# Attention into an MLP on one core: q and k of two batches turned to token slots before a full-width transpose, and the beacon keys of a batch by one operation

## The chip, the cores and the metric

The kernel runs on 1 core of one Trainium2 chip. The metric is the device time of one launch in microseconds (us); the median of 3 runs before the change is 348.35 us (348.26 to 348.68). The engines of a core are TensorE (PE), VectorE (DVE), ScalarE (ACT), GpSimd (POOL) and SyncE (SP), the last used here to issue DMAs. POOL issues DMAs too, those that convert fp32 to bf16 on the way among them.

## The reference

Attention over 8 batches, 8 heads, 576 tokens of 64 elements, with 16 beacon keys and values ahead of the token keys, which every query may see; the token part is causal. The result, as 4608 tokens of 512, goes through an MLP with a squared ReLU.

```python
k_all = np.concatenate([beacon_k, k], axis=2)          # 16 + 576 keys
v_all = np.concatenate([beacon_v, v], axis=2)
scores = scale * np.matmul(q, k_all.transpose(0, 1, 3, 2))
causal[:, Nb:] = np.triu(np.ones((S, S), dtype=bool), k=1)
scores = np.where(causal, -1000000000.0, scores)
a = softmax(scores)
x = np.matmul(a, v_all)                                # then (B*S, H*D)
h = x @ w_in
r = np.maximum(h, 0.0)
out = (r * r) @ w_out
```

## The kernel before

Every step is a small operation (`Op`) with a name, the engine or engines that may run it, a planned duration, a priority and the operations that it needs. When the kernel is built, a planner (`Order.run`) plays them through: whenever an engine is free it starts the ready operation with the lowest priority number. What comes out is one fixed order per engine. On the chip each engine keeps its order and waits by semaphores. The planner also deals out PSUM's 8 banks in classes with limits (`tp`, the transposes, has 2 banks at most), staging buffers `stg` (8), and buffers `pt` (4) for the exponentials. It adds 0.096 us where PE changes between "full", "rows" and "columns" operations (`mode`).

The work of a batch goes by pairs of heads, `pr` = 0 to 3:

- Keys and queries are needed with the 64 elements of a head on partitions, two heads of a pair on 128: `kT` and `qT`. In batches 0 to 2 (`b < NPE`), `add_strided` makes them on PE. POOL's DMAs (line 463) put k and q as bf16 into `ks` and `qs`, parts of `qk_area`: 96 partitions, and on each partition 6 token slots per head (token = 6 x partition + slot). A `tp` operation then transposes, for k and for q, each slot of each head by itself (line 480): 96x64 in, 64x96 out, the second head to the upper 64 partitions, 24 matmuls a pair, mode "columns". Line 476 adds the pair's beacon keys. `ek` (VectorE) copies keys and beacon keys to `kT`, `eq` (VectorE or ScalarE) copies `qT`, bringing the tokens back in order.
- The beacon keys are loaded for all heads by SP (line 445) and cast by VectorE (line 448), in `add_beacon`.
- From batch 3 on, q and k are loaded by SP to `stg`, cast by POOL and transposed by DMA. Ahead of batches 3 and 4 POOL clears parts of `qk_area` (lines 381 and 382), once the transposes of batches 1 and 2 are read out.
- `qk` (line 584) multiplies keys and queries in two row halves of the array, ScalarE takes the exponential (line 597), VectorE masks by `tri` (lines 607 and 611), `av` (line 627) multiplies by the values `vb`, VectorE normalises to `xn` (lines 642 and 643). Of batch 1, the value loads are issued by POOL, not SP.
- `xT` is the transpose of `xn`, by PE in batches 0 and 1 (line 691), by DMA later.
- The MLP runs in 9 chunks of 512 tokens: line 755 (w_in), relu on ScalarE (772) or VectorE (774), square on VectorE (781), line 792 (w_out), a copy by ScalarE to `osb` (355), and SP's store. MLP matmuls have high priority numbers, so they fill PE when no attention operation is ready. A gate holds a pair's attention back until the MLP is far enough along.

Line 357 is the helper `copy_on`, through which copies and casts of VectorE and POOL go. The weights are loaded by POOL: `w_in` (716) before batch 1's q and k, `w_out` (725) after batch 1's values.

Of the kernel before, what the change touches and what calls it, by code (L numbers as in the profile page):

```python
# [9 lines left out]
FP32 = mybir.dt.float32  # L10
BF16 = mybir.dt.bfloat16
# [77 lines left out]
class Order:  # L89
# [147 lines left out]
def kernel(  # L237
# [11 lines left out]
    nc = tc.nc  # L249
    B, H, S, D = q.shape  # L250
    Nb = beacon_k.shape[2]
    HP = H // 2
# [14 lines left out]
    def sb(name, shape, dt):  # L267
        return pool.tile(shape, dt, name=name)
# [5 lines left out]
    stg = [sb(f"stg{i}", [128, H, D], FP32) for i in range(NSTG)]  # L274
    NP = 96
    NS = S // NP
# [25 lines left out]
    ps = psum.tile([128, 8, 512], FP32, name="ps")  # L302
# [4 lines left out]
    def bank(op, k=0):  # L307
        return ps[:, op.held[k], :]
# [19 lines left out]
    add = order.add  # L328
# [16 lines left out]
    ident_op = add("ident", "POOL", 0.6, lambda e: make_identity(nc, ident), prio=-199.8)  # L345
# [7 lines left out]
    def copy_on(e, dst, src):  # L353
        if e == "ACT":
            nc.scalar.copy(dst, src)  # L355
        else:
            eng[e].tensor_copy(dst, src)  # L357
# [3 lines left out]
    cast = {}  # L361
    trans = {}
    qk_ops = {}
# [77 lines left out]
        deps += [o for p in range(HP * (b - 2), HP * (b - 1)) for o in qk_ops[p]]  # L441
        trans[b, x] = [add(f"tr{b}{x}", "SP", 3.8, emit, prio=prio, deps=deps, dma=3.2)]

    def add_beacon(b, prio):
        ld = add(f"bkl{b}", "SP", 0.65, lambda e: [nc.sync.dma_start(
            out=bkf[b % 2], in_=beacon_k[b].transpose([1, 0, 2]))], prio=prio, dma=0.1,
                 deps=[cast[b - 1, "bk"]] if b else [])
        cast[b, "bk"] = add(f"bkc{b}", "DVE", 0.4, lambda e: nc.vector.tensor_copy(bks[b % 2], bkf[b % 2]), prio=prio,
                               deps=[ld])
        return cast[b, "bk"]  # L450

    def add_strided(b, prio):
        loads = {}
        bk = add_beacon(b, prio)
        after = [w_ops["in", 3]] if b == 1 else [strided[b - 1][HP - 1, "q"]] if b else []
        free = trans[b - 2, "q"] + trans[b - 2, "k"] if b >= 2 else []
# [12 lines left out]
        strided[b] = loads  # L469
        for pr in range(HP):  # L470
            h = slice(2 * pr, 2 * pr + 2)
            box = {}

            def emit_tp(e, pr=pr, h=h, box=box):
                pp = pair(box["t"]).bitcast(BF16)
                nc.tensor.transpose(pp[:, 1, 0:Nb], bks[b % 2][:, h, :], ident[0:Nb, 0:Nb])  # L476
                for half, at, t in ((1, Nb, ks), (0, 0, qs)):
                    for u in range(NS):
                        for hj in range(2):
                            nc.tensor.transpose(pp[64 * hj:64 * hj + 64, half, at + u * NP:at + (u + 1) * NP],  # L480
                                                t[b % 2][:, 2 * pr + hj, u, :], ident[0:NP, 0:NP])
# [21 lines left out]
            trans[b, "q"].append(eq)  # L503


    class Phase:
# [397 lines left out]
```

## Time and profile before

| | |
|---|---|
| median of 3 runs | 348.35 us (348.26 to 348.68) |
| the profiled execution | 349.44 us, span 347.7 us |
| granted TensorE clock | 1.00 |
| line 480, half-width transposes | 288 matmuls |
| line 476, beacon transposes | 12 matmuls |
| DMA | 49.50 MB, HBM 134 GB/s over the span |

The span runs from the first to the last instruction that the profile shows; the time of a run has some 1.7 us more around it. Busy time of PE is a sum of overlapping matmuls taken together; the distance from start to start tells what a matmul takes up on the engine. In a timeline a row merges neighbours of one kind: start, time from the first start to the last end, engine, line, operation, shape and count. A releaser in brackets is what ended the engine's idle time before that row.

### The profile page before, as it was taken

The numbers are of one execution on the slowest core, as the hardware profiler recorded it, in microseconds if no ns is written. First come the engines' busy times: TensorE is split into PE (matmuls) and PEld (weight loads), VectorE is DVE, ScalarE is ACT, GpSimd is POOL, SyncE is SP. The second block draws the span as 40 slices with busy tenths as digits, with TensorE's granted clock in tenths as the row PEclk, the third lists the DMA queues.
The fourth block names the chain that finished last, engine by engine and source line by source line (L and its number), as shares of the span: only waits on it lengthen the run. The fifth ranks groups of instructions, "written<-read, shape, count | busy, mean of one in ns | idle before, by whom it ended". The sixth has DMA issues, their size and how long they took to land.

```text
span 347.7 us, 7270 instructions
## 1 busy us (share of the span) xinstructions
PE 331.8 (95%) x2944; PEld 177.7 (51%) x2980; DVE 150.2 (43%) x306; ACT 202.3 (58%) x311; POOL 84.8 (24%) x132
## 2 busy tenths in 40 slices
PE   3799999999999999999999999999999999999995
PEld 2568765554544444544446874454454444444442
DVE  5466683448722464256523772266323302301300
ACT  2678893497854775577655765677536416614611
POOL 8273740357242046105520452000000000000000
PEclk9999999999999999999999999999999999999999
DMA  7989999899978999899986999750014011011002
GB/s 99 188 126 205 221 206 215 192 248 213 201 150 194 208 207 204 130 237 201 238 173 135 215 242 227 120 139 2 3 60 128 2 60 60 2 60 60 3 15 105
DMA packets 137010, 49.50 MB, mean 142 GB/s; under 512 B 123344, under 2 KB 132048, under 8 KB 136976
## 3 DMA queue, kind: packets, MB, share of 16 engines
q1 hardware_dynamic: 127472, 40.09, 55.7%
q0 software_dynamic: 9504, 8.95, 16.0%
q8 instruction: 23, 0.38, 0.5%
q14 instruction: 11, 0.09, 0.1%
HBM read 37.22 MB, written 9.44 MB: 134 GB/s over the span
## 4 chain that ended last, share of the span: by engine, by line
PE 92%; DMA 3%; issue 2%; ACT 1%; DVE 1%; POOL 0%; SPq 0%; ACTq 0%; POOLq 0%
PE ps L755 36%; PE ps L792 36%; PE ps L627 9%; PE ps L584 8%; DMA stg<-in_v_dram 2%; PE ps L480 1%; DMA qk_area<-in_q_dram 1%; PE ps L691 1%; ACT pt L597 1%; DVE pt L607 1%; PE ps L476 0%; DVE g L774 0%; POOL vb L357 0%; ACT osb L355 0%; POOL qk_area L463 0%
## 5 line engine op out<-in xcount | busy, mean ns | idle before, releaser
L755 PE MATMUL ps<-xT,w_in 128*128 128x512 bf16 (+3 forms) x688 | 132.8, 340 | 1.2 <-issue 0.5
L792 PE MATMUL ps<-w_out,g 128*128 128x512 bf16 x556 | 127.8, 379 | 2.0 <-issue 1.4
L597 ACT ACTIVATE pt<-ps 128x832 bf16<-128x832 f32 (+4 forms) x128 | 103.8, 869 | 43.9 <-PE ps L584 41.9
L755 PEld LDWEIGHTS <-w_in 128*128 128x128 bf16 x704 | 65.1, 98 | 56.1 <-issue 5.3
L772 ACT ACTIVATE g<-ps 128x512 bf16<-128x512 f32 (+2 forms) x128 | 71.7, 560 | 36.0 <-PE ps L755 34.7
L792 PEld LDWEIGHTS <-g 128*128 128x128 bf16 x576 | 53.9, 98 | 66.7 <-issue 4.8
L781 DVE TENSOR_TENSOR g<-g 128x1024 bf16<-128x1024 bf16 (+2 forms) x80 | 51.8, 649 | 71.8 <-ACT g L772 71.0
L355 ACT COPY osb<-ps 128x512 f32<-128x512 f32 x36 | 21.1, 587 | 47.4 <-PE ps L792 41.5
L357 POOL CAST vb<-stg 128x512 bf16<-128x512 f32 (+1 forms) x38 | 26.8, 714 | 78.2 <-DMA stg<-in_v_dram 74.0
L607 DVE TENSOR_TENSOR pt<-pt,tri 128x1024 bf16<-128x1024 bf16 (+1 forms) x36 | 24.8, 693 | 45.4 <-ACT pt L597 44.0
L357 POOL CAST qk_area<-stg 128x512 bf16<-128x512 f32 (+2 forms) x50 | 33.2, 676 | 28.2 <-DMA stg<-in_k_dram 14.8
L627 PEld LDWEIGHTS <-pt 128*128 128x128 bf16 (+1 forms) x960 | 34.9, 100 | 8.6 <-issue 1.6
L627 PE MATMUL ps<-vb,pt 128*128 128x65 bf16 (+1 forms) x960 | 36.8, 197 | 1.0 <-POOL vb L357 0.5
L584 PE MATMUL ps<-qT,kT 64*128 64x80 bf16 (+6 forms) x400 | 36.4, 291 | 1.0 <-ACT pt L597 1.0
L774 DVE TENSOR_SCALAR g<-ps 128x512 bf16<-128x512 f32 (+2 forms) x32 | 19.6, 612 | 19.3 <-PE ps L755 18.9
L643 DVE TENSOR_TENSOR xn<-ps,rcp 128x640 bf16<-128x640 f32 (+2 forms) x36 | 27.0, 751 | 1.3
L584 PEld LDWEIGHTS <-kT 64*128 64x128 bf16 x400 | 13.0, 97 | 21.1 <-issue 17.5
L642 DVE RECIPROCAL rcp<-ps 128x10 f32<-128x10 f32 (+2 forms) x36 | 7.6, 211 | 32.4 <-PE ps L627 32.2
L355 ACT COPY qT<-ps 128x576 bf16<-128x576 bf16 x12 | 7.8, 651 | 11.2 <-PE ps L480 11.2
L480 PE MATMUL ps<-ident,qk_area 96*64 96x96 bf16 x288 | 11.1, 233 | 2.7 <-DMA qk_area<-in_q_dram 1.2
L357 DVE COPY kT<-ps 128x16 bf16<-128x16 bf16 (+1 forms) x24 | 9.9, 453 | 5.2 <-PE ps L480 5.0
L480 PEld LDWEIGHTS <-qk_area 96*64 96x64 bf16 x288 | 8.6, 126 | 4.0 <-DMA qk_area<-in_q_dram 2.1
(31 smaller groups left out, 57.2 us busy)
## 6 DMA issues: line engine op xcount, KB each, us to landing
out_dram<-osb SPq DMA_DIRECT2D x17, 512.0 KB, 3.2
stg<-in_v_dram SPq DMA_DIRECT2D x21, 256.0 KB, 5.7
stg<-in_q_dram SPq DMA_DIRECT2D x20, 256.0 KB, 4.9
stg<-in_k_dram SPq DMA_DIRECT2D x15, 256.0 KB, 5.1
w_in<-in_moe_w_in_dram POOLq DMA_DIRECT2D x4, 512.0 KB, 8.7
w_out<-in_moe_w_out_dram POOLq DMA_DIRECT2D x4, 512.0 KB, 10.9
stg<-in_v_dram SPq DMA_DIRECT2D x7, 224.0 KB, 5.2
qk_area<-in_k_dram POOLq DMA_DIRECT2D x4, 288.0 KB, 12.4
```

What stands on the lines that cost most here:

```text
L355: nc.scalar.copy(dst, src)
L357: eng[e].tensor_copy(dst, src)
L480: nc.tensor.transpose(pp[64 * hj:64 * hj + 64, half, at + u * NP:at + (u + 1) * NP], t[b % 2][:, 2 * pr + hj, u, :], ident[0:NP, 0:NP])
L584: nc.tensor.matmul(st[:, hj, at:at + t1 - t0], kT[b % 2][hp, pr, 128 * c:128 * c + 128], qT[b % 2][hp, pr, t0:t1], start=True, stop=True,)
L597: nc.scalar.activation(pt[take_pt.held[0]][:, :, off:off + width], pair(box["qk"], k)[:, :, 0:width], AF.Exp, bias=0.0, scale=scale)
L607: nc.vector.tensor_tensor(out=d, in0=d, in1=tri[:, m0:m0 + m, :][:, None].to_broadcast([128, 2, m, 128]), op=ALU.min)
L627: nc.tensor.matmul(a[:, hj, (t - tl[0]) * (D + 1):(t - tl[0] + 1) * (D + 1)], P[0:rr, hj, o:o + 128], vb[b % 2][0:rr, c, h, :], start=(c = ...
L643: nc.vector.tensor_tensor(out=xn[b % 2].rearrange("p t (h d) -> p h t d", d=D)[:, 2 * pr:2 * pr + 2, tl[0]:tl[0] + nt], in0=a[:, :, :, 0:D ...
L755: nc.tensor.matmul(h[:, lo - spans[0][0]:hi - spans[0][0]], w_in_sb[:, mc, ft * 128:(ft + 1) * 128], xT[:, mc, lo % RING:lo % RING + hi - lo],
L772: nc.scalar.activation(dst, h, AF.Relu, bias=0.0, scale=1.0)
L781: nc.vector.tensor_tensor(out=d, in0=d, in1=d, op=ALU.mult)
L792: nc.tensor.matmul(o, G[:, fc, ts * 128:(ts + 1) * 128], w_out_sb[:, fc, :], start=(fc == 0), stop=(fc == NFT - 1))
```

## The change

Three things change in `add_beacon` and `add_strided`.

1. In batches 1 and 2, VectorE rearranges k and q of each pair before the transpose (`spin`): from head, slot, element to slot, head, element, so that one slot of both heads lies in 128 neighbouring columns. The target is a spare buffer for pair 0 and, for the others, the place of the pair before, which has been rearranged by then. PE then transposes a slot of both heads at once: 12 matmuls of 96x128 instead of 24 of 96x64, mode "full". Batch 0 keeps the 24.
2. The beacon keys of all four pairs of a batch are turned by one operation `tpb` on PE: four matmuls of the 128-row buffer `bks` (rows beyond 16 are zero, by a memset at the start) against 16 columns of the identity, into one PSUM bank. `ekb` copies all of it to `kT` at once. `ek` has no beacon copy any more.
3. Batch 0's beacon keys are staged in a `stg` buffer, loaded by SP and cast by VectorE as before. Those of batches 1 and 2 are loaded by POOL with the conversion in the DMA, into the one `bks`; the load waits for the batch before to be transposed, and stands between the batch's first k and q loads.

The planned durations of `tp` and `ek` change accordingly.

```diff
-    bkf = [sb("bkf", [Nb, H, D], FP32)] * 2
-    bks = [sb(f"bks{i}", [Nb, H, D], BF16) for i in range(2)]
+    bks = sb("bks", [128, H, D], BF16)
+    spare = {x: sb(f"spare{x}", [NP, NS * 2 * D], BF16) for x in "kq"}
...
+    nc.vector.memset(bks, 0.0)
...
-    def add_beacon(b, prio):
-        ld = add(f"bkl{b}", "SP", 0.65, lambda e: [nc.sync.dma_start(
-            out=bkf[b % 2], in_=beacon_k[b].transpose([1, 0, 2]))], prio=prio, dma=0.1,
-                 deps=[cast[b - 1, "bk"]] if b else [])
-        cast[b, "bk"] = add(f"bkc{b}", "DVE", 0.4, lambda e: nc.vector.tensor_copy(bks[b % 2], bkf[b % 2]), prio=prio,
-                               deps=[ld])
-        return cast[b, "bk"]
+    def add_beacon(b, prio, behind):
+        if b == 0:
+            def emit_load(e):
+                return [nc.sync.dma_start(out=stg[ld.held[0]][0:Nb], in_=beacon_k[b].transpose([1, 0, 2]))]
+
+            ld = add(f"bkl{b}", "SP", 0.65, emit_load, prio=prio, dma=0.1, take=("stg", "stg", [1]))
+            bk = add(f"bkc{b}", "DVE", 0.4, lambda e: nc.vector.tensor_copy(bks[0:Nb], stg[ld.held[0]][0:Nb]),
+                     prio=prio, deps=[ld], give=ld)
+        else:
+            bk = add(f"bkl{b}", "POOL", 0.65, lambda e: [nc.gpsimd.dma_start(
+                out=bks[0:Nb], in_=beacon_k[b].transpose([1, 0, 2]))], prio=prio + 0.05, dma=0.1,
+                behind=behind, deps=[tpb_ops[b - 1]])
+        box = {}
+
+        def emit_tpb(e):
+            for pr in range(HP):
+                nc.tensor.matmul(bank(box["t"])[:, Nb * pr:Nb * pr + Nb], bks[:, 2 * pr:2 * pr + 2, :],
+                                 ident[:, 0:Nb], start=True, stop=True)
+
+        def emit_ekb(e):
+            nc.vector.tensor_copy(kT[b % 2][:, :, 0:Nb],
+                                  bank(box["t"])[:, 0:HP * Nb].rearrange("p (g n) -> p g n", n=Nb))
...
+        tpb = add(f"tpb{b}", "PE", 0.2, emit_tpb, prio=100.0 * HP * b - 195, deps=[bk, ident_op] + busy,
+                  take=("ps", "tp", [1]))
...
+        ekb_ops[b] = add(f"ekb{b}", "DVE", 0.14, emit_ekb, prio=-201.0, deps=[tpb], give=tpb)
...
+                    def emit_spin(e, h=h, x=x, t=t, blocks=blocks):
+                        copy_on(e, blocks[x].rearrange("p s (h d) -> p h s d", h=2), t[b % 2][:, h])
+
+                    spin[x].append(add(f"spin{b}{x}{pr}", "DVE", 0.45, emit_spin, prio=prio + pr,
+                                       deps=[loads[pr, x]] + spin[x][-1:] + ([tps[b - 1, 0]] if pr == 0 and b > 1 else [])))
...
-                nc.tensor.transpose(pp[:, 1, 0:Nb], bks[b % 2][:, h, :], ident[0:Nb, 0:Nb])
...
-                        for hj in range(2):
-                            nc.tensor.transpose(pp[64 * hj:64 * hj + 64, half, at + u * NP:at + (u + 1) * NP],
-                                                t[b % 2][:, 2 * pr + hj, u, :], ident[0:NP, 0:NP])
+                        cols = slice(at + u * NP, at + (u + 1) * NP)
+                        if b:
+                            nc.tensor.transpose(pp[:, half, cols], blocks[x][:, u, :], ident[0:NP, 0:NP])
+                        else:
+                            for hj in range(2):
+                                nc.tensor.transpose(pp[64 * hj:64 * hj + 64, half, cols],
+                                                    t[b % 2][:, 2 * pr + hj, u, :], ident[0:NP, 0:NP])
...
-            tp = add(f"tp{b}.{pr}", "PE", 1.0 if b else 1.3, emit_tp, prio=100.0 * (HP * b + pr) - 190,
-                     deps=[bk, loads[pr, "k"], loads[pr, "q"], ident_op] + busy, take=("ps", "tp", [2]), mode="columns")
+            tp = add(f"tp{b}.{pr}", "PE", 0.55 if b else 1.0, emit_tp, prio=100.0 * (HP * b + pr) - 190,
+                     deps=([spin["k"][pr], spin["q"][pr]] if b else [loads[pr, "k"], loads[pr, "q"]]) + [ident_op] + busy,
+                     take=("ps", "tp", [2]), mode="full" if b else "columns")
...
-                copy_on(e, kT[b % 2][:, pr, 0:Nb], pp[:, 1, 0:Nb])
...
-            ek = add(f"ek{b}.{pr}", "DVE", 0.85, emit_k, prio=-200.0, deps=[tp])
+            ek = add(f"ek{b}.{pr}", "DVE", 0.7, emit_k, prio=-200.0, deps=[tp])
...
-            qk_deps = [trans[b, "k"][pr], trans[b, "q"][pr]]
+            qk_deps = [trans[b, "k"][pr], trans[b, "q"][pr], ekb_ops[b]]
```

More of the change, by code (lines that the diff above doesn't have):

```diff
@@ L442, in add_trans @@
         trans[b, x] = [add(f"tr{b}{x}", "SP", 3.8, emit, prio=prio, deps=deps, dma=3.2)]
-    def add_beacon(b, prio):
-        ld = add(f"bkl{b}", "SP", 0.65, lambda e: [nc.sync.dma_start(
-            out=bkf[b % 2], in_=beacon_k[b].transpose([1, 0, 2]))], prio=prio, dma=0.1,
-                 deps=[cast[b - 1, "bk"]] if b else [])
-        cast[b, "bk"] = add(f"bkc{b}", "DVE", 0.4, lambda e: nc.vector.tensor_copy(bks[b % 2], bkf[b % 2]), prio=prio,
-                               deps=[ld])
-        return cast[b, "bk"]
+    tpb_ops = {}
+    ekb_ops = {}
+    def add_beacon(b, prio, behind):
[17 more added lines that the diff above has]
+                                  bank(box["t"])[:, 0:HP * Nb].rearrange("p (g n) -> p g n", n=Nb))
+        busy = [o for pr in range(HP) for o in qk_ops[HP * (b - 2) + pr]] if b >= 2 else []
+        tpb = add(f"tpb{b}", "PE", 0.2, emit_tpb, prio=100.0 * HP * b - 195, deps=[bk, ident_op] + busy,
+                  take=("ps", "tp", [1]))
+        box["t"] = tpb
+        tpb_ops[b] = tpb
+        ekb_ops[b] = add(f"ekb{b}", "DVE", 0.14, emit_ekb, prio=-201.0, deps=[tpb], give=tpb)
     def add_strided(b, prio):
         loads = {}
-        bk = add_beacon(b, prio)
         after = [w_ops["in", 3]] if b == 1 else [strided[b - 1][HP - 1, "q"]] if b else []
+        add_beacon(b, prio, after)
         free = trans[b - 2, "q"] + trans[b - 2, "k"] if b >= 2 else []
@@ L469, in add_strided @@
         strided[b] = loads
+        spin = {"k": [], "q": []}
         for pr in range(HP):
@@ L472, in add_strided, with block @@
             box = {}
-            def emit_tp(e, pr=pr, h=h, box=box):
+            def block(x):
+                if pr == 0:
+                    return spare[x][:, :].rearrange("p (s w) -> p s w", s=NS)
+                return (ks if x == "k" else qs)[b % 2][:, 2 * pr - 2:2 * pr].rearrange(
+                    "p h s d -> p (h s d)").rearrange("p (s w) -> p s w", s=NS)
+            blocks = {x: block(x) for x in "kq"}
+            if b:
+                for x, t in (("k", ks), ("q", qs)):
+                    def emit_spin(e, h=h, x=x, t=t, blocks=blocks):
+                        copy_on(e, blocks[x].rearrange("p s (h d) -> p h s d", h=2), t[b % 2][:, h])
+                    spin[x].append(add(f"spin{b}{x}{pr}", "DVE", 0.45, emit_spin, prio=prio + pr,
+                                       deps=[loads[pr, x]] + spin[x][-1:] + ([tps[b - 1, 0]] if pr == 0 and b > 1 else [])))
@@ L475, in emit_tp @@
+            def emit_tp(e, pr=pr, h=h, box=box, blocks=blocks):
                 pp = pair(box["t"]).bitcast(BF16)
-                nc.tensor.transpose(pp[:, 1, 0:Nb], bks[b % 2][:, h, :], ident[0:Nb, 0:Nb])
-                for half, at, t in ((1, Nb, ks), (0, 0, qs)):
+                for half, at, x, t in ((1, Nb, "k", ks), (0, 0, "q", qs)):
                     for u in range(NS):
-                        for hj in range(2):
-                            nc.tensor.transpose(pp[64 * hj:64 * hj + 64, half, at + u * NP:at + (u + 1) * NP],
-                                                t[b % 2][:, 2 * pr + hj, u, :], ident[0:NP, 0:NP])
+                        cols = slice(at + u * NP, at + (u + 1) * NP)
+                        if b:
+                            nc.tensor.transpose(pp[:, half, cols], blocks[x][:, u, :], ident[0:NP, 0:NP])
[3 more added lines that the diff above has]
+                                                    t[b % 2][:, 2 * pr + hj, u, :], ident[0:NP, 0:NP])
@@ L486, in add_strided @@
+            tps[b, pr] = tp
             box["t"] = tp
@@ L503, in add_strided @@
             trans[b, "q"].append(eq)
+    tps = {}
     class Phase:
```

## The prediction

> **What bounds the kernel now.** I read the page first, for the share of each engine and the chain that ended last.
>
> ```profile
> span 347.7 us, 7270 instructions
> PE 331.8 (95%) x2944; PEld 177.7 (51%) x2980; DVE 150.2 (43%) x306; ACT 202.3 (58%) x311; POOL 84.8 (24%) x132
> PE   3799999999999999999999999999999999999995
> PE 92%; DMA 3%; issue 2%; ACT 1%; DVE 1%; POOL 0%; SPq 0%; ACTq 0%; POOLq 0%
> ```
>
> TensorE (PE) is busy for 331.8 of 347.7 us, the chain is 92% PE, and only the first two slices and the last show PE idle. From about 20 us on the kernel is a queue of TensorE work. What shortens that queue should arrive at the end; what lengthens another engine costs only where PE has to wait for it.
>
> The change touches three stretches: batch 0 at the start, batch 1's transposes around 37 to 45 us, batch 2's around 63 to 74 us. So I cut the span into windows (columns: PE, weight loads, DVE, ACT, POOL busy us; granted clock; DMA share; GB/s).
>
> ```profile
> 8.70:17.40 8.70, 6.67 (x96) 4.41 (x92) 3.81 (x11) 5.78 (x9) 1.84 (x3) 1.00 1.01 188
> 26.00:35.00 9.00, 8.98 (x122) 7.77 (x122) 5.76 (x18) 7.39 (x17) 3.20 (x4) 1.00 1.27 205
> 35.00:46.00 11.00, 11.00 (x171) 7.79 (x170) 8.14 (x20) 9.63 (x20) 8.20 (x13) 1.00 1.17 219
> 46.00:57.00 11.00, 10.89 (x133) 6.41 (x133) 7.33 (x18) 7.88 (x13) 1.79 (x3) 1.00 1.27 204
> 57.00:68.00 11.00, 10.89 (x154) 6.55 (x154) 4.92 (x10) 4.16 (x7) 3.20 (x5) 1.00 1.04 206
> ```
>
> PE is full in all but the first of these, at full clock. VectorE (DVE), to which the change gives work, has 11.00 - 8.14 = 2.86 us free in 35 to 46 us, its busiest stretch, and about 6 us in 57 to 68.
>
> **What one transpose of a pair costs now.** The timeline of PE around the first two of batch 1 (start, time from first start to last end, engine, line, shape, count):
>
> ```profile
> 35.76 1.21 PE L755 MATMUL ps<-xT,w_in 128*128 128x272 bf16 x9
> 36.89 0.18 PE L476 MATMUL ps<-ident,bks 16*128 16x16 bf16 x1
> 37.00 0.70 PE L480 MATMUL ps<-ident,qk_area 96*64 96x96 bf16 x24
> 37.63 1.56 PE L755 MATMUL ps<-xT,w_in 128*128 128x272 bf16 x12
> ...
> 39.24 0.70 PE L480 MATMUL ps<-ident,qk_area 96*64 96x96 bf16 x24
> 39.87 0.38 PE L584 MATMUL ps<-qT,kT 64*128 64x496 bf16 x2
> ```
>
> Starts, not ends, give the price, since matmuls overlap. The two L755 groups differ by 3 matmuls and 0.35 us, so one follows the other by 0.117 us, and one lasts 1.21 - 8 x 0.117 = 0.27 us. The last of the nine therefore starts at 35.76 + 0.94 = 36.70, and the next full-array matmul could have started at 36.82. The beacon transpose starts at 36.89, 0.07 to 0.09 late. It takes a slot of 0.11 us, until 37.00. From there to the next L755 at 37.63 are 0.63 us. A pair's transpose thus keeps PE for 37.63 - 36.82 = 0.81 us.
>
> Of the 0.63 us, the 24 half-width transposes need this much (min/median/max ns of one; L691 for later):
>
> ```profile
> L627 PE MATMUL ps<-vb,pt x420: 190/194/262, 14.5 to 109.8; 128*128 128x65 bf16 x140
> L480 PE MATMUL ps<-ident,qk_area x288: 206/206/290, 4.5 to 73.7; 96*64 96x96 bf16 x144
> ...
> L691 PE MATMUL ps<-ident,xn x40: 199/218/313, 16.7 to 68.5; 128*128 128x128 bf16 x24, 112*128 112x112 bf16 x8, 80*128 80x80 bf16 x8
> ```
>
> (0.70 - 0.206)/11 = 0.045 us for each of 12 steps, so two heads' halves already go side by side. 12 steps are 0.54 us; the remaining 0.09 us at the way out, like that at the way in, stands where PE goes from full-width to 64-column work and back.
>
> **The same transposes in full width.** No row shows 96x128. Two neighbours do, both full-width, each with its own 128-column weight load: 65 moving columns and 128.
>
> ```profile
> 51.30 1.08 PE L627 MATMUL ps<-vb,pt 128*128 128x65 bf16 x30
> ...
> 31.29 1.39 PE L755 MATMUL ps<-xT,w_in 128*128 128x240 bf16 x12
> 32.52 0.31 PE L691 MATMUL ps<-ident,xn 128*128 128x128 bf16 x3
> 32.74 0.47 PE L755 MATMUL ps<-xT,w_in 128*128 128x240 bf16 x3
> ```
>
> L627: (1.08 - 0.194)/29 = 0.0306 us a step. L691 from its start to the next group's: 0.22/3 = 0.073 at most, and about 0.056 a step if the last lasts its shortest 0.199. So 12 transposes cost between 0.37 us (12 x 0.0306) and 0.88 us (12 x 0.073). I take 96 columns midway between 65 and 128, 0.043 us a step, 0.52 us, close to the 0.045 of L480's pairs. L691's transposes also show no lost time beside L755: the last of the 12 before them starts near 32.42, and they follow after 0.10 us, a normal step.
>
> So the transpose of a pair goes from 0.81 to 0.52 us: 0.29 us less, eight times. Two of the eight have a row-split matmul (L584) as a neighbour, the one at 39.24 above and this one:
>
> ```profile
> 72.70 0.48 PE L584 MATMUL ps<-qT,kT 64*128 64x336 bf16 x8
> 73.11 0.18 PE L476 MATMUL ps<-ident,bks 16*128 16x16 bf16 x1
> ```
>
> There one switch of about 0.09 us stays. Gain: 8 x 0.29 - 2 x 0.09 = 2.14 us. The beacon keys of a batch come back as four full-width matmuls with 16 columns; the nearest row is L627's 0.031 us, so 0.12 us a batch, 0.25 us for two (0 to 0.43 if each costs today's 0.11 less the switch). **PE queue: 1.9 us shorter** (1.0 longer with 0.073 a step, 3.1 shorter with 0.0306).
>
> The Trainium skill (TensorE: Matmul & The Clock Gate, section on LDWEIGHTS) says that a weight load takes the number of its columns over 1.2 GHz, whatever the rows; that is 107 ns for 128 columns, and 12 loads would be 1.28 us, an estimate by that page; its section on Fast Weight Load makes such loads about twice as fast. L627's 30 steps of 0.0306 us, each with 128 columns, speak against it here; what it would do is a rival below.
>
> **VectorE's new work.** 16 copies of 96 x 768 bf16 between SBUF buffers, two per pair, one each for k and q. Nearest rows, by shape (count | busy us, mean ns):
>
> ```profile
> L357 DVE COPY kT<-ps 128x16 bf16<-128x16 bf16 x12 | 1.9, 160 | 5.2 <-PE ps L480 5.0
> L448 DVE CAST bks<-bkf 16x512 bf16<-16x512 f32 x3 | 1.3, 420 | 1.5 <-DMA bkf<-in_beacon_k_dram 1.5
> L357 DVE COPY xT<-ps 128x576 bf16<-128x576 bf16 x3 | 1.4, 454 | 2.1 <-PE ps L691 2.1
> L357 DVE COPY xT<-ps 128x240 bf16<-128x240 bf16 x3 | 0.7, 271 | 0.0
> L357 DVE CAST vb<-stg 128x512 bf16<-128x512 f32 x1 | 0.4, 429 | 1.0 <-DMA stg<-in_v_dram 1.0
> ```
>
> The xT copies give (454 - 271)/336 = 0.54 ns an element over 0.14 us fixed, so 0.56 us for 768; the cast fits that line (0.42). If bf16 inside SBUF goes at twice that pace it is 0.35 us. I take 0.45, with 0.35 and 0.56 as ends: 3.6 us a batch. Taken away: four beacon copies of 0.16 us a batch and a 0.42 us cast; added: one 64-column copy, about 0.18 us. In 35 to 46 us VectorE would then have 8.14 + 3.6 - 0.6 + 0.2 = 11.3 us if every copy fell there. They need not:
>
> ```profile
> 35.92 0.74 POOL L402 DMA_DIRECT2D stg<-in_v_dram  x1 [0.61 <-DMA qk_area<-in_q_dram]
> 7.49 1.39 PE L480 MATMUL ps<-ident,qk_area 96*64 96x96 bf16 x24 [1.19 <-DMA qk_area<-in_k_dram]
> 63.16 0.18 PE L476 MATMUL ps<-ident,bks 16*128 16x16 bf16 x1
> ```
>
> POOL's first row shows batch 1's first q in place before 35.92 us, so its copies can use the 3.24 idle us of 26 to 35 as well as the 3.67 of 46 to 57. The planner that writes the order books the copies and fills PE with L755 and L792 work meanwhile. Behind a copy in VectorE's queue stand relu (L774), square (L781), mask (L607) and the kT copies; PE, ScalarE and PSUM banks wait for those. I charge 0.4 us for places where PE stands (0 to 1.9, all of the gain).
>
> **Batch 0 and the queues.** The beacon cast comes behind a new memset, and the first pair waits until the beacon's bank is read. The second row above covers it: PE stands 1.19 us before the second pair anyway, and a delay of that length costs nothing. Without that cover it would cost its length. The beacon load of batch 1 leaves SP's queue ahead of batch 0's v loads: 32 KB at 188 GB/s, 0.17 us off a DMA-bound start at best; I book 0. Two beacon loads move into POOL's queue, between a k and a q load, each pushing the later q and k loads, then v (batch 1) and w_out, by the same 0.2 us; POOL's issue costs another 0.7 us each, while it waits for landings anyway. Batch 2's beacon load also waits for batch 1's beacon matmuls, which stand ahead of batch 1's transposes (36.89); behind it in POOL's queue are batch 2's q and k loads, first used at 63.16, and then the v casts. I book 0 (-0.2 to +0.5).
>
> **Sum.** -1.9 + 0.4 = -1.5 us. The profiled execution took 349.44 us with its span of 347.7, so 1.7 lie around the span; it becomes 347.9. The median of the runs is 348.35, 1.1 lower; the same cut gives 346.8.
>
> **Rivals.** *Given back at PE.* The order is fixed; PE cannot pass a transpose whose copy is late. 1.9/8 = 0.24 us of waiting at each pair eats the gain: 348.3. For it: VectorE's 8.14 of 11, and two copies in a row per pair. Against: the planner books them, and PE was idle for only 0.11 us in each window of 46 to 68.
>
> *Slower: VectorE and GpSimd block each other.* Rows of both engines:
>
> ```profile
> 39.11 2.23 POOL L725 DMA_DIRECT2D w_out<-in_moe_w_out_dram  x3 [1.24 <-DMA qk_area<-in_q_dram]
> 41.32 1.95 POOL L357 CAST vb<-stg 128x512 bf16<-128x512 f32 x3
> 41.45 0.79 DVE L781 TENSOR_TENSOR g<-g 128x480 bf16<-128x480 bf16 x1
> 46.87 0.39 DVE L781 TENSOR_TENSOR g<-g 128x480 bf16<-128x480 bf16 x1
> ...
> 74.79 0.69 DVE L607 TENSOR_TENSOR pt<-pt,tri 128x1024 bf16<-128x1024 bf16 x1 [0.23 <-ACT pt L597]
> 75.59 6.12 POOL L357 CAST qk_area<-stg 128x512 bf16<-128x512 f32 x10
> 80.18 2.08 DVE L607 TENSOR_TENSOR pt<-pt,tri 128x1024 bf16<-128x1024 bf16 x1
> ```
>
> Under POOL's casts a square takes 0.79 instead of 0.39 us and a mask 2.08 instead of 0.69. If each copy is stretched by the same 0.4 us to 0.85, batch 1's eight are 6.8 us: 8.14 + 6.8 - 0.4 = 14.5 in 11, 3.5 over; what 26 to 35 doesn't take stalls relu and squares, and PE. With 3 us lost and 1.9 gained it is 349.5. It decides from (2.86 + 0.4)/8 = 0.41 us a copy if all fall into that window, from about 0.8 if they spread over all three. Against: until 41 us POOL issues DMAs (L725) and casts nothing. The Trainium skill (SBUF — State Buffer, Who interferes with whom) says that a VectorE copy in a two-port mode locks the port pair that GpSimd uses, and the later one waits; the two stretched rows look like it, though they are two-input operations.
>
> *Wide loads are not hidden.* The page's row of such loads:
>
> ```profile
> L755 PEld LDWEIGHTS <-w_in 128*128 128x128 bf16 x704 | 65.1, 98 | 56.1 <-issue 5.3
> ```
>
> If each 128-column load stood in PE's way for its 98 ns, 12 would be 1.18 us instead of 0.81: 8 x 0.37 + 0.25 = 3.2 slower, 351.5. L627 is against it. The rule of the Trainium skill named above would do this.
>
> *The switch stays.* If 96 rows counted as another array shape, both 0.09 us would remain: gain 1.9 - 6 x 0.18 = 0.8, less 0.4: 347.9. L691 has transposes of 112 and 80 rows among its own and shows no such loss, so it is unlikely.
>
> **Chances.** Forecast 0.63; given back 0.17; blocking 0.13; switch stays 0.04; wide loads 0.03. A measurement here tells about 0.2%, 0.7 us, from no change. Faster by more: 0.63 plus a little of the switch case, 0.64. Within: 0.19. Slower: 0.17. The forecast alone spans 345.6 (0.035 a step: 8 x 0.39 - 0.43 = 2.7 us, nothing lost) to 347.6 (0.8 us left); the range reaches to the other cases, up to 349.2, where half of the blocking case and the wide loads are left out.
>
> **What would show it.** Right: L480 as 96*128, x12 per pair, steps near 0.043 us, next group at once; PE busy smaller; PE's full windows still full; copies of 0.35 to 0.56 us. Wrong: PE idle before L480 with VectorE's copy as releaser, steps above 0.07 us, copies near 0.85 us under POOL's casts, or a hole before 50 us where L755's work has run out and w_out is late.

## The result and the profile after

The changed kernel takes 351.97 us (median of 4 runs, 350.56 to 352.87) where the kernel before, run on the same chip, takes 348.36 (348.26 to 348.68): a ratio of 1.0092, 95% interval 1.0076 to 1.0108. It is slower by 3.6 us by the medians, 3.2 by the ratio; forecast were 1.5 us faster, and 351.97 lies above the range. The profiled execution took 352.09 us with a span of 350.4, 2.7 more than the span before.

The page of the changed kernel, the lines that answer to those of before, with the row of the granted clock:

```profile
span 350.4 us, 7092 instructions
PE 329.7 (94%) x2849; PEld 176.8 (50%) x2884; DVE 153.4 (44%) x308; ACT 204.1 (58%) x315; POOL 85.2 (24%) x134
PE   3789989999999959999999999999999999999995
PEclk9999999999999969999999999999999999999999
PE 75%; DMA 10%; SPq 6%; POOL 4%; issue 3%; DVE 1%; ACT 1%; POOLq 0%; DVEq 0%; ACTq 0%
```

PE's busy time is 2.1 us lower. That says little: a second profiled execution of the same kernel (number 11 below) has 331.9 us, as much as before. But the row of slices has a 5 at the fifteenth slice (123 to 131 us), where there was a 9, the clock falls to 6 in the same slice, and the chain that ended last is only 75% PE: 10% is now a DMA and 6% SyncE's queue (SPq). The view of waits on PE names the transfer (line, what was waited for: us, times, longest):

```profile
PE ps L633 <- DMA kT<-qk_area: 4.0, 1, 4.0
...
PE ps L740 <- DVE xn L692: 0.8, 1, 0.8
```

The upper one is new, and the longest behind the start of the kernel: batch 4's first scores (L633, L584 before) wait 4.0 us for the DMA transpose of batch 4's keys. This is 50 us behind the last line that the change edits. PE's timeline around it, after:

```profile
113.27 0.58 PE L633 MATMUL ps<-qT,kT 64*128 64x496 bf16 x4
...
121.32 1.03 PE L804 MATMUL ps<-xT,w_in 128*128 128x512 bf16 x3
126.35 0.98 PE L633 MATMUL ps<-qT,kT 64*128 64x496 bf16 x4 [4.00 <-DMA kT<-qk_area]
127.27 4.67 PE L804 MATMUL ps<-xT,w_in 128*128 128x512 bf16 x12
131.87 0.48 PE L633 MATMUL ps<-qT,kT 64*128 64x336 bf16 x8
```

The same places before:

```profile
117.09 0.58 PE L584 MATMUL ps<-qT,kT 64*128 64x496 bf16 x4
...
126.11 0.58 PE L584 MATMUL ps<-qT,kT 64*128 64x496 bf16 x4
126.62 2.76 PE L755 MATMUL ps<-xT,w_in 128*128 128x512 bf16 x12
129.32 0.48 PE L584 MATMUL ps<-qT,kT 64*128 64x336 bf16 x8
```

Read the pairs of starts. At 113.27 the changed kernel is 3.82 us **ahead**. At 126.35 it is 0.24 behind, and at 131.87 it is 2.55 behind, although PE no longer waits in between: the 4 + 12 matmuls after the wait take 5.52 us from start to start, against 3.21 before. The windows say why (columns as in the prediction, the granted clock being the figure behind POOL):

```profile
124.00:126.00 2.00, 0.00 (x0) 0.00 (x0) 0.00 (x0) 0.00 (x0) 0.61 (x1) 0.58 1.08 245
...
130.00:131.00 1.00, 1.00 (x4) 0.30 (x2) 0.00 (x0) 0.10 (x1) 0.52 (x1) 0.50 1.29 214
132.00:134.00 2.00, 2.00 (x16) 0.93 (x13) 0.87 (x3) 1.87 (x3) 1.49 (x3) 1.00 1.35 205
```

The clock is halved while PE stands and for some 5 us behind. So the hole costs about 4.0 us of standing and 2.3 us of half-speed work: 6.3 us, of a lead of 3.8, which leaves the 2.5. (Part of that lead belongs to this execution and not to the change; number 1 below shows it.)

Why was kT late? SyncE's queue after:

```profile
106.20 4.38 SPq L435 DMA_TRANSPOSE qT<-qk_area  x1
110.62 1.21 SPq L403 DMA_DIRECT2D stg<-in_k_dram  x2
...
112.43 4.98 SPq L403 DMA_DIRECT2D stg<-in_v_dram  x5
117.51 0.66 SPq L864 DMA_DIRECT2D out_dram<-osb  x1
118.26 1.61 SPq L402 DMA_DIRECT2D stg<-in_beacon_k_dram  x1
...
120.45 3.78 SPq L435 DMA_TRANSPOSE kT<-qk_area  x1
```

and before:

```profile
105.72 2.60 SPq L402 DMA_DIRECT2D stg<-in_k_dram  x3
...
110.16 5.61 SPq L434 DMA_TRANSPOSE qT<-qk_area  x1
115.87 3.05 SPq L434 DMA_TRANSPOSE kT<-qk_area  x1
```

Before, all k loads go first, then the two transposes back to back. After, the q transpose has slipped in ahead of the last two k loads, and occupies the queue for 4.38 us; the k loads leave late, and by the time their casts on GpSimd are done the k transpose stands behind the beacon values and five v loads, a store and two loads of the next batch. The casts were done at 116.09 us:

```profile
115.48 0.61 POOL L358 CAST qk_area<-stg 80x512 bf16<-80x512 f32 x1 [0.58 <-DMA stg<-in_k_dram]
```

so 4.4 us of queueing follow until 120.45. The arithmetic closes. Before, kT landed at 121.04 us (the DMA's own record) for a use at 126.11: 5.07 us to spare. After, it lands at 126.30, 5.26 later, and PE is there 3.8 us sooner: 5.07 - 5.26 - 3.8 = -4.0. Nobody edited this order. The kernel's planner, given other durations for batch 0, 1 and 2, wrote it.

### The profile page after: what moved, and what is told of

It is laid out like the page before. It is cut to its first block, busy times and chain, and to the rows that moved or that the text cites. A ratio compares the mean times of both kernels' runs of the same rounds, so it can differ in the third digit from the quotient of the medians.

```text
span 350.4 us, 7092 instructions
## 1 busy us (share of the span) xinstructions
PE 329.7 (94%) x2849; PEld 176.8 (50%) x2884; DVE 153.4 (44%) x308; ACT 204.1 (58%) x315; POOL 85.2 (24%) x134
## 4 chain that ended last, share of the span: by engine, by line
PE 75%; DMA 10%; SPq 6%; POOL 4%; issue 3%; DVE 1%; ACT 1%; POOLq 0%; DVEq 0%; ACTq 0%
PE ps L841 31%; PE ps L804 30%; PE ps L676 6%; PE ps L633 6%; DMA stg<-in_v_dram 3%; DMA qk_area<-in_q_dram 2%; SPq L723 2%; DMA stg<-in_q_dram 2%; DMA kT<-qk_area 2%; SPq L403 2%; SPq L435 1%; POOL qk_area L358 1%; POOL qk_area L489 1%; DMA stg<-in_k_dram 1%; PE ps L740 1%
## 5 line engine op out<-in xcount | busy, mean ns | idle before, releaser
L804 PE MATMUL ps<-xT,w_in 128*128 128x512 bf16 (+3 forms) x690 | 134.4, 343 | 1.0 <-issue 0.3
L841 PE MATMUL ps<-w_out,g 128*128 128x512 bf16 x555 | 127.3, 379 | 2.1 <-issue 1.4
L804 PEld LDWEIGHTS <-w_in 128*128 128x128 bf16 x704 | 66.0, 98 | 57.5 <-issue 7.8
L841 PEld LDWEIGHTS <-g 128*128 128x128 bf16 x576 | 54.1, 98 | 66.3 <-issue 4.4
L830 DVE TENSOR_TENSOR g<-g 128x1024 bf16<-128x1024 bf16 (+2 forms) x80 | 52.7, 662 | 72.2 <-ACT g L821 71.6
L358 POOL CAST qk_area<-stg 128x512 bf16<-128x512 f32 (+2 forms) x50 | 34.4, 699 | 53.0 <-DMA stg<-in_k_dram 40.3
L633 PE MATMUL ps<-qT,kT 64*128 64x80 bf16 (+6 forms) x400 | 36.6, 291 | 4.9 <-DMA kT<-qk_area 4.0
L358 POOL CAST vb<-stg 128x512 bf16<-128x512 f32 (+1 forms) x38 | 24.8, 661 | 57.2 <-DMA stg<-in_v_dram 53.9
L676 PEld LDWEIGHTS <-pt 128*128 128x128 bf16 (+1 forms) x960 | 33.3, 98 | 8.4 <-DVE pt L656 1.7
L676 PE MATMUL ps<-vb,pt 128*128 128x65 bf16 (+1 forms) x960 | 35.1, 194 | 0.3 <-DVE pt L656 0.3
L692 DVE TENSOR_TENSOR xn<-ps,rcp 128x640 bf16<-128x640 f32 (+2 forms) x36 | 27.0, 750 | 1.3
L633 PEld LDWEIGHTS <-kT 64*128 64x128 bf16 x400 | 12.9, 97 | 24.0 <-issue 16.1
L358 DVE COPY kT<-ps 128x576 bf16<-128x576 bf16 x12 | 9.0, 750 | 4.9 <-PE ps L523 3.1
L660 DVE TENSOR_TENSOR pt<-pt,tri 80x160 bf16<-80x160 bf16 x32 | 9.0, 281 | 0.0
L526 PE MATMUL ps<-ident,qk_area 96*64 96x96 bf16 x96 | 5.3, 282 | 2.9 <-DMA qk_area<-in_q_dram 1.8
```

Of the source, the lines that this page charges most:

```text
L633: nc.tensor.matmul(st[:, hj, at:at + t1 - t0], kT[b % 2][hp, pr, 128 * c:128 * c + 128], qT[b % 2][hp, pr, t0:t1], start=True, stop=True,)
L676: nc.tensor.matmul(a[:, hj, (t - tl[0]) * (D + 1):(t - tl[0] + 1) * (D + 1)], P[0:rr, hj, o:o + 128], vb[b % 2][0:rr, c, h, :], start=(c = ...
L692: nc.vector.tensor_tensor(out=xn[b % 2].rearrange("p t (h d) -> p h t d", d=D)[:, 2 * pr:2 * pr + 2, tl[0]:tl[0] + nt], in0=a[:, :, :, 0:D ...
L804: nc.tensor.matmul(h[:, lo - spans[0][0]:hi - spans[0][0]], w_in_sb[:, mc, ft * 128:(ft + 1) * 128], xT[:, mc, lo % RING:lo % RING + hi - lo],
L830: nc.vector.tensor_tensor(out=d, in0=d, in1=d, op=ALU.mult)
L841: nc.tensor.matmul(o, G[:, fc, ts * 128:(ts + 1) * 128], w_out_sb[:, fc, :], start=(fc == 0), stop=(fc == NFT - 1))
```

## The experiments

The ratios below are to the kernel before, run beside it on the same chip, at 348.8 to 349.0 us. Planned durations, not only work, were changed by the edit, so the two have to be taken apart.

**1. Pin the order back.** The changed kernel, with the q transpose booked behind the issue of the last k load:

```diff
-        trans[b, x] = [add(f"tr{b}{x}", "SP", 3.8, emit, prio=prio, deps=deps, dma=3.2)]
+        trans[b, x] = [add(f"tr{b}{x}", "SP", 3.8, emit, prio=prio, deps=deps, dma=3.2,
+                           behind=[load_chain[-NT - 1]])]
```

> The changed kernel; SyncE may issue batch b's q transpose only after it has issued the last k load of that batch. On paper this moves entries of SyncE's order alone; every other engine keeps the order of the changed kernel. Theory 1 (the loss is one entry of SyncE's order: batch 4's q transpose ahead of the last two k loads, so that the kT transpose comes late; PE stands 4.2 us and then works at half clock for 4.7 us, 2.4 us more): the hole at 122 us goes, PE busy in 110 to 150 us comes back to about 39.4, and the time is 352.0 - 6.5 = 345.5 us, between 345 and 346.5, faster than before. Theory 2 (VectorE's 16 copies and GpSimd hold each other up, and the casts and so the transposes of batch 4 are late for that, whatever SyncE's order): kT is late still, 350 us or more. Theory 3 (batch 4's data come late from the DMA queues, by the moved beacon loads): as theory 2, 350 or more.

347.17 us (345.40 to 347.46), ratio 0.9938 (0.9918 to 0.9958). Only SyncE's order differs from the changed kernel's; the other engines' orders are the same. (The line holds for every batch from 3 on and moves a few later entries too.) Its queue, and the window over the place of the hole:

```profile
105.50 1.43 SPq L403 DMA_DIRECT2D stg<-in_k_dram  x2
107.11 4.42 SPq L435 DMA_TRANSPOSE qT<-qk_area  x1
...
113.34 3.76 SPq L435 DMA_TRANSPOSE kT<-qk_area  x1
```

```profile
110.00:150.00 40.00, 40.00 (x334) 18.96 (x332) 17.11 (x31) 25.72 (x39) 12.92 (x18) 1.00 1.04 204
```

PE is full for 40 of 40 us at full clock. One line of order turns 0.9% slower into 0.6% faster: the order of SyncE's queue, and not the copies or the transposes, made the change a loss. 345.5 was expected. By the ratios 0.7 us are missing (345.5 is 0.9918 of 348.36), and the interval just covers that. But the traces show an error in the expectation: it takes the whole hole off the time, and so the whole lead of 3.82 us for the change's own. Number 1 has the same order of PE and is only 2.07 us ahead of the kernel before at that place (117.09 there):

```profile
115.02 0.58 PE L634 MATMUL ps<-qT,kT 64*128 64x496 bf16 x4
```

The difference arises at the start. The same 48 products with the values in the changed kernel, in number 1 and in the kernel before:

```profile
20.84 1.63 PE L676 MATMUL ps<-vb,pt 128*128 128x65 bf16 x48
```

```profile
21.29 2.84 PE L677 MATMUL ps<-vb,pt 128*128 128x65 bf16 x48
```

```profile
22.29 2.85 PE L627 MATMUL ps<-vb,pt 128*128 128x65 bf16 x48
```

Less 0.194 us for the last one, that is 0.031 us a step in the first row and 0.057 in the third. So PE starts at about half its later pace, and in the profiled execution of the changed kernel it came to the full pace earlier than in the others. (The column of the granted clock has 1.00 here in all three and does not show this.) For the changed kernel such a start is worth nothing: kT landed at 126.30 us in this execution and at 126.34 in that of number 11, where PE was 3.17 us ahead (113.92); a greater lead makes a longer wait.

**2. Put the fault into the old kernel.** The kernel before, with batch 4's next-to-last k load booked behind its q transpose:

```diff
+            if b == 4:
+                load_chain[-NT - 2].behind.append(trans[b, "q"][0])
```

> The kernel before, nothing of the change in it; only SyncE's order differs: batch 4's load of k3 (and what follows) comes behind that batch's q transpose, as it does in the changed kernel. Theory 1: a hole before the first scores of batch 4 opens here too, with a clock of 0.5 behind it: PE needs kT at 126 us, and the kT transpose, planned 5.2 us later than before, would land at 121 + 5 to 8 us; so 0 to 3 us idle, and 350 to 354 us. Theories 2 and 3: no copies and no moved load, so 348.4 us, as before.

350.98 us (350.23 to 353.19), ratio 1.0063 (1.0040 to 1.0087). Its waits and its windows around the hole:

```profile
PE ps L584 <- DMA kT<-qk_area: 2.3, 1, 2.3
```

```profile
126.00:128.40 2.40, 0.14 (x3) 0.02 (x4) 1.07 (x2) 0.60 (x1) 0.00 (x0) 0.94 0.83 178
128.40:131.00 2.60, 2.60 (x9) 0.72 (x10) 0.00 (x0) 1.83 (x2) 1.68 (x3) 0.50 0.95 217
```

The hole opens in a kernel that has none of the edit. kT lands at 128.33, 7.29 later than in the kernel before, and 5.07 - 7.29 = -2.2 is the wait that is seen. In this execution, the slowest of six (353.19 us, mean granted clock 0.993), the clock is halved behind it too. The other five list 0.998 to 1.000, as kernels without a hole do, and take 350.23 to 351.24 us: they are slower than the kernel before without a fall of the clock.

**3. and 4. Take the half clock away, leave the wait.** The changed kernel with PE kept at work in the hole by 16, then by 10 extra matmuls of 128x512 ahead of batch 4's first scores (their result is overwritten):

```diff
+                if p == 16 and i == 0:
+                    for _ in range(16):     # second kernel: 10
+                        nc.tensor.matmul(pair(box["qk"], 0)[:, 0, :], w_in_sb[:, 0, 0:128],
+                                         w_in_sb[:, 1, 0:512], start=True, stop=True)
```

> The changed kernel with 16 extra matmuls of 128x512 on weights ahead of batch 4's first scores, into the PSUM bank which those then overwrite: 3.5 us of work that needs no data from DMA, placed where PE stands. It leaves kT's lateness as it is. If the half clock after the hole costs 2.4 us by itself, the time is about 352.0 - 2.4 = 349.6 us, and the clock stays at 1.00. If the clock does not depend on PE standing, or costs nothing, it is 352, and 355.5 if the extra work delayed the scores by its whole length.

> As e5, with 10 extra matmuls (2.2 us) in place of 16 (3.5 us), which in e5 outlasted a hole that was 2.4 us long in that execution. If standing PE costs the clock, and the half clock some 2 us, the time is now the changed kernel's less 1.5 to 2.4 us, 1.002 to 1.005 of before, and the clock stays full after the hole; if only the hole itself counts, it is the changed kernel's, 1.009.

With 16: 351.24 us (349.66 to 352.02), 1.0054 (1.0033 to 1.0074). The clock stays at 1.00, but the extra work ends only about a microsecond after kT has landed (126.42), which costs that time. With 10 it ends before, and the timeline of PE shows what is left:

```profile
123.44 2.32 PE L630 MATMUL ps<-w_in 128*128 128x512 bf16 x10
126.73 0.58 PE L637 MATMUL ps<-qT,kT 64*128 64x496 bf16 x4 [0.97 <-DMA kT<-qk_area]
127.25 2.76 PE L808 MATMUL ps<-xT,w_in 128*128 128x512 bf16 x12
```

The twelve L808 take 2.76 us, as before, and no longer 4.67. The time is 350.46 us (348.99 to 352.97), 1.0054 (1.0032 to 1.0077). Against the changed kernel's 1.0092 that is 0.4%, or 1.3 us; against its repetition below 1.8. This is a little less than was expected (1.002 to 1.005), and one of the eight executions (352.97 us) still lists a clock of 0.994. It is compatible with the 2.3 us of the profiled execution: a quarter to a third of the hole's price is clock, the rest is the wait.

**5. The beacon part alone.** Change and pin, but with no copies and with the 24 half-width transposes in all batches:

```diff
-                    if b:                      # copies by VectorE
+                    if False:
...
-                        if b:                  # 96x128 transposes
+                        if False:
...
-            tp = add(f"tp{b}.{pr}", "PE", 0.55 if b else 1.0, ...
+            tp = add(f"tp{b}.{pr}", "PE", 1.0, ...
```

> The beacon part of the change alone, with SyncE's order held as in e1: one beacon operation per batch, the moved loads, but no copies on VectorE and 24 half-width transposes a pair in all three batches. By the slots of the profile: 8 x 0.11 us less of PE in batches 1 and 2, 2 x 0.11 us more, 0.7 us faster than before, 347.7 us (347.2 to 348.4), if theory 1 holds. Theory 3 expects late data here too, 350 or more; theory 2 expects no loss, since there are no copies.

346.87 us (346.26 to 348.22), 0.9932 (0.9916 to 0.9948), where 347.7 was expected. This was a surprise: without the copies and the full-width transposes, which are the heart of the change, the kernel is as fast as with them (0.9938).

**6. The start by order alone.** The kernel before with only the planned durations of batch 0 altered as the change alters them, and the pin:

```diff
-            tp = add(f"tp{b}.{pr}", "PE", 1.0 if b else 1.3, emit_tp, ...
+            tp = add(f"tp{b}.{pr}", "PE", 1.0, emit_tp, ...
-            ek = add(f"ek{b}.{pr}", "DVE", 0.85, emit_k, prio=-200.0, deps=[tp])
+            ek = add(f"ek{b}.{pr}", "DVE", 0.85 if b else 0.7, emit_k, prio=-200.0, deps=[tp])
```

> The kernel before with its own work in full (beacon transposes by pair, 24 half-width transposes, no copies); only two planned durations of batch 0 are those of the change (transpose 1.0 for 1.3, kT copy 0.7 for 0.85), and SyncE's order of batch 4 is held as in e1. This makes PE's order at the start that of the changed kernel: the first scores of pair 2 stand ahead of the first values product, which waits for v. Theory 1a (the 1.0 us by which e1 and e4 lead at 25 us comes from that place in PE's order, not from less work): 1.0 us faster than before, about 347.4 against 348.4, and the lead is there at the first relu. Rival 1b (it comes from the beacon work taken out of batch 0 and from one load less ahead of v): no lead, 348.4.

347.80 us (347.39 to 348.66), 0.9975 (0.9964 to 0.9986): 0.9 us, with no work added or removed. Its PE at 15 us, and that of the kernel before:

```profile
15.14 0.84 PE L585 MATMUL ps<-qT,kT 64*128 64x240 bf16 x8
15.90 0.84 PE L628 MATMUL ps<-vb,pt 128*128 128x65 bf16 x12
```

```profile
15.33 0.71 PE L627 MATMUL ps<-vb,pt 128*128 128x65 bf16 x10 [0.54 <-POOL vb L357]
15.97 0.80 PE L584 MATMUL ps<-qT,kT 64*128 64x240 bf16 x8
```

The scores go ahead of a product that still waits for a cast of v. The changed kernel has the same order. How much of the 0.9 us arises here is not shown: the two durations alter the order further on as well. Between batch 0's last transpose of `xn` and batch 1's first pair stand 44 matmuls with w_in (L756), where the kernel before has 36.

**7. and 8. What the copies cost.** Number 1 with copies and full-width transposes in batch 2 only (`if b == 2` for `if b`); and number 1 with every copy made twice (which gives the same data):

```diff
-                        copy_on(e, blocks[x].rearrange("p s (h d) -> p h s d", h=2), t[b % 2][:, h])
+                        for _ in range(2):
+                            copy_on(e, blocks[x].rearrange("p s (h d) -> p h s d", h=2), t[b % 2][:, h])
```

> As e1, but only batch 2 has the copies and the full-width transposes; batch 1 keeps 24 half-width ones. Theory 2a (in 35 to 49 us VectorE is short of time: the copies of batch 1 take back there, as standing PE and late masks, what their transposes save): as fast as e1 or faster, 0.990 to 0.994 of before, VectorE less busy in 35 to 46 us and no hole near 48 us. Rival 2b (every full-width pair is worth its 0.3 us): 1.2 us slower than e1, 0.997.

> As e1, every copy made twice into the same place, 32 instead of 16; all engines keep e1's order. Theory 2a: VectorE has no room in 35 to 49 us, eight copies more of 0.35 to 0.6 us there cost 2 to 4 us of standing PE, 1.000 to 1.006 of before; in 57 to 74 us they cost little. Rival 2b (VectorE off the path): as e1, 0.994.

Batch 2 only: 346.60 us (345.44 to 347.75), 0.9931 (0.9914 to 0.9948), not told apart from number 1. Doubled: 350.67 us (350.16 to 351.36), 1.0061 (1.0048 to 1.0075). The same two windows of number 1, of batch 2 only, and of the doubled kernel:

```profile
35.00:46.00 11.00, 10.74 (x128) 8.76 (x126) 10.26 (x24) 10.06 (x22) 8.81 (x14) 1.00 1.15 219
46.00:57.00 11.00, 10.31 (x128) 5.68 (x127) 5.53 (x13) 7.70 (x11) 1.28 (x2) 1.00 1.29 204
```

```profile
35.00:46.00 11.00, 11.00 (x175) 7.95 (x172) 7.56 (x17) 9.75 (x21) 8.83 (x14) 1.00 1.17 218
46.00:57.00 11.00, 10.89 (x128) 6.55 (x129) 5.30 (x13) 6.77 (x11) 1.83 (x3) 1.00 1.28 203
```

```profile
35.00:46.00 11.00, 9.43 (x104) 7.16 (x102) 10.79 (x27) 8.34 (x18) 8.74 (x14) 1.00 1.16 211
```

Read PE beside DVE. Without batch 1's copies VectorE is busy for 7.56 of 11 us and PE stands 0.11 us in both windows together; with them 10.26 and 0.95; with twice as many 10.79, and PE stands 1.57 in the first window alone. The 16 further copies cost 0.0123 of the time, 4.3 us, 0.27 us each. So most of a further copy is paid by PE, and not only where VectorE is full: in 57 to 68 us the doubled kernel's VectorE is busy for 8.67 of 11 us, and yet PE stands for 1.30 us (0.01 in number 1), 0.8 of them for a kT copy ahead of a transpose. The doubled kernel's copies were planned at the old 0.45 us, so part of its price is that the order did not know of them.

**9. and 10. Let PE have other work there.** Number 1, and number 7, with the w_out loads booked at dma=2.5 instead of 3.15 us, so that the planner brings the work that needs them (L841) forward.

> As e1 (the whole change, SyncE's order of batch 4 held), with the planner's booking of a w_out load at 2.5 us of DMA time in place of 3.15; the chip's landings are 2.5 us apart. The planner may then start w_out products about 1 us earlier, 43.9 in place of 45.0 in its own time, where PE stands near 48 us in e1. If PE's standing there is only a matter of order, 0.5 to 0.9 us less than e1: 0.991 of before. If VectorE's lack of time is what counts, as e1 or worse, since the same copies and masks are in the way: 0.994.

> As e8 (copies and full-width transposes in batch 2 alone), with w_out booked at 2.5 us as in e10. VectorE has room in 35 to 49 us here, so there is little standing to take away: 0.991 to 0.994 of before by either theory; a check that the order of w_out products alone moves the time by no more than the 1 us that separates e1, e4 and e6.

347.43 us (345.60 to 348.46), 0.9955 (0.9938 to 0.9971), and 348.39 us (346.60 to 349.07), 0.9981 (0.9964 to 0.9998): no gain in the first, a loss in the second. In the first, PE stands less at one place and more at others, where it waits for VectorE (L358's xT, 0.6 us, and qk_area, 0.4 us); that speaks for a VectorE short of time and against a mere lack of work for PE. The second is 1.7 us slower than number 7; its expectation failed. In its profiled execution PE waits 0.7 us for the DMA transpose of batch 3's keys, which number 7's does not; the rest has no cause that a run shows.

**11. The changed kernel once more,** as it is.

> The changed kernel once more, timed beside e10 and e11 on one chip, for the size of the hole against e1's ratio of 0.994: 1.007 to 1.011 of before if the first timing holds; the difference to e1 is then 4.5 to 6 us (theory 1: 4.2 of standing and 2.4 of half clock, less where the start is later).

352.32 us (351.72 to 352.96), 1.0105 (1.0087 to 1.0122), with the same wait (3.4 us in its profiled execution). Between it and number 1 lie 0.0167, 5.8 us; between the first measurement and number 1, 0.0154, 5.4 us. That is the price of the queue's order.

Numbers 1, 5 and 7 (0.9938, 0.9932, 0.9931) beat both kernels by at least 0.4% and can't be told apart.

## Why the prediction was wrong, by its own steps

**PE's queue: -1.9 us, right.** PE's timeline after, at batch 1's first pair:

```profile
36.27 0.42 PE L523 MATMUL ps<-ident,sparek 96*128 96x96 bf16 x6
36.52 0.42 PE L523 MATMUL ps<-ident,spareq 96*128 96x96 bf16 x6
36.78 1.40 PE L804 MATMUL ps<-xT,w_in 128*128 128x272 bf16 x11
```

From 36.27 to 36.78 a pair takes 0.51 us (forecast 0.52), with a step of 0.0425 (0.043) and no time lost on the way in or out. So the wide loads are hidden, and the switch does not stay: both rivals fall. The estimate by the Trainium skill (TensorE: Matmul & The Clock Gate, LDWEIGHTS), 12 loads of 107 ns one after the other, falls with the first: L523's loads last 98 ns each, near that figure, but they overlap, and a step is 0.0425 us.

**Copies of 0.45 us: right in size, wrong in price.** Undisturbed they take 0.34 to 0.35 us, the lower end; the mean is 0.44 over all 16. But the step that follows, "I charge 0.4 us for places where PE stands", was mis-sized. The windows after:

```profile
35.00:46.00 11.00, 10.69 (x147) 8.49 (x145) 10.15 (x24) 10.38 (x22) 8.55 (x14) 1.00 1.16 214
46.00:57.00 11.00, 10.11 (x124) 5.49 (x123) 4.39 (x11) 7.12 (x10) 1.62 (x3) 1.00 1.28 203
```

PE stands for 1.2 us in them against 0.11 before: 1.1 us, the larger part at 47 us, where L740 waits 0.8 us for a chain on VectorE (L692). So this term was 0.4 and measured 1.1 (0.8 in number 1: 0.95 against 0.11). A hole before 50 us was among the signs of error that the prediction named, though with a late w_out as its cause, and here it is VectorE. Number 5 and number 7 show the consequence: what copies and wide transposes save on PE is taken back, within what these runs can tell. That is the rival "given back at PE", and it held; but with the rest of the edit at -0.6% it alone would not have made the kernel slower. I had counted VectorE's idle time of a window as room. Idle time in an order written beforehand is room only where the copy comes before something that PE needs later, and not sooner.

**VectorE and GpSimd block each other: real and small.** In number 1's kernel a copy takes 1.21 us under GpSimd's casts and 0.34 behind them. VectorE's rows, then GpSimd's:

```profile
41.29 1.21 DVE L358 COPY qk_area<-qk_area 96x768 bf16<-96x768 bf16 x1
...
44.18 0.34 DVE L358 COPY qk_area<-qk_area 96x768 bf16<-96x768 bf16 x1
```

```profile
40.05 2.23 POOL L358 CAST vb<-stg 128x512 bf16<-128x512 f32 x3
```

The mean of 0.44 says how few copies it met. The rival gave 349.5 us, the result lies above, and its mechanism is not the cause.

**The step that failed: "I book 0" for batch 0 and the queues.** It fails twice. With batch 0's durations the order of PE changed, at the start and behind it, worth -0.9 us (number 6). And the prediction followed SyncE's and POOL's queues only through the stretches that the edit touches. It took the rest of the order as given, although the durations that the planner reads were among the edited lines. The planner then put one transpose of SyncE's queue ahead of two loads, 50 us later, at a price of 5.4 to 5.8 us (number 11 against number 1). No rival named it. In the planner's own time batch 4's scores follow kT without trouble; on the chip the time from the q transpose to the k transpose was 14.25 us where the planner had 10.95.

Without that the forecast would have held: 0.9938 of 348.36 is 346.2 us, inside the range. But it would have held by luck, by errors that work against each other: -0.9 from PE's order, and at VectorE +0.4 to +0.7 by the standing in the windows, or more by number 5. And by numbers 5 and 6 most of that gain comes from the beacon keys and the new order, not from what the sum credited. How the rest of number 5's gain, 0.9975 to 0.9932, divides between beacon matmuls on PE and VectorE's copies saved isn't settled: the sum gives 0.6 us for the first, and the runs 1.5 with an uncertainty of about 0.7. Which of the edited durations moved the transpose was not run either. The planner itself, which needs no chip, says that it took all three: with any single one set back in the changed kernel (1.0 for the pair transposes of batches 1 and 2, 1.3 for batch 0's, or 0.85 for `ek`) it puts both loads ahead of the transpose again.

## What to carry to other kernels

Where a planner writes the order from durations, an edit of durations is an edit of every queue behind it: before forecasting, look for transfers with a small reserve between landing and use (here 5.1 us for kT) and ask what a lead of PE and another order of the queue each take from it. Compare the queues of the two kernels entry by entry before believing that a slower kernel has a worse idea; one entry moved back may show the gain. And idle time of an engine in a window is no room for work that PE waits for: double the added work and see what one more costs. A lead read from one execution can belong to that execution: compare a second one with the same order before taking it for the change's.

## What the runs showed of the hardware

A wait of PE can be paid twice. In the changed kernel the clock was down after about 2 us of standing (from 122.35; the window 124 to 126 has 0.58), and it stayed at 0.50 up to 131 us. In the profiled execution of the swapped old kernel (number 2) a wait of 2.27 us was enough, and the window behind it has 0.50, while the other five executions of that kernel show no such fall; the 0.97 us in the profile of number 4 were not enough. The Trainium skill (TensorE: Matmul & The Clock Gate, the table of clock states and its free-running window) puts the fall after an idle window of about 3.4 us. A window that runs freely would explain that one kernel loses its clock in one execution and not in another; but standing of 2.27 us lies below that figure, and here the measurement decides.

PE also starts slowly: 0.057 us a step for 48 products at 22 us, 0.031 later. When that ends differs between executions with the same order of PE; between the changed kernel's and number 1's it makes up most of the difference of the leads, 3.82 and 2.07 us: 1.2 us in the row of those products alone.

A copy of 96 x 768 bf16 inside SBUF takes 0.34 us alone and up to 1.21 us under GpSimd's casts, more than the twofold stretch of the squares before. The Trainium skill (SBUF — State Buffer, Who interferes with whom) has such copies and GpSimd excluding each other at a shared port; the rows agree.
